# Prologue of a two-stage mixing kernel: weight additions on TensorE, a third output buffer, split loads of the mixer input, and steps of the next group begun early

## The chip, the cores and the metric

The program runs on one core of a Trainium2 chip. The core has five engines that run their own instruction queues: TensorE (PE in the profile; PEld is its weight load), VectorE (DVE), ScalarE (ACT), GpSimd (POOL) and SyncE (SP). SP, ACT and POOL issue the DMAs, which run on 16 DMA engines. Times are device microseconds of one execution; the metric is the median over several executions. Lower is better.

## The reference

Two blocks run one after the other on x of shape (8, 3008, 256), float32.

```python
X = np.fft.rfft(x, axis=1)                         # block 1: global filter
y = np.fft.irfft(X * (filt_r + 1j * filt_i)[None], n=3008, axis=1)
xt = y.transpose(0, 2, 1)                          # block 2: token and channel mixing
h = np.maximum(xt @ w_tok1, 0.0) @ w_tok2          # (3008, 256), (256, 3008)
u = y + h.transpose(0, 2, 1)
h2 = np.maximum(u @ w_ch1, 0.0) @ w_ch2            # (256, 1536), (1536, 256)
return u + h2
```

`filt_r` and `filt_i` are (1505, 256). x and the filters are float32; the four mixer weights arrive as float64 and are rounded to float32 on the chip.

## The kernel before

**The filter.** N = 3008 is written as 47 x 64, and the transform is done as two matmul passes. `dft(bs)` is a generator that runs it for a group of batches; one `next` is one step. Its first 12 steps per batch are `a_unit`s: load an x tile (`x_load`, two DMAs on SP), one matmul with the table `wa`, a copy to `t1` on ACT, a write to the scratch tensor `z_tmp` from ACT's queue. Then come 32 units, one per frequency row k: `b_unit` multiplies a `t2` tile (read back from `z_tmp`) by a table `wb`, and VectorE multiplies the result by the filter (L436 to L440); one step later `bi_unit` transforms back (L448), and ACT copies the result to a `t3` tile, which is written to the scratch tensor `g_tmp` (L453, L458). Rows go in chunks of KC = 2. `load(c)` fetches what chunk c needs: the table (L411, SP), the filter rows (`filt_load`, L196 to L203), and `t2` (L416, SP). For the first group it puts one copy of `filt_r` on SP and the other, with `filt_i`, on POOL; filt_r is wanted on both halves of the partitions. `load(c + 2)` is called in the unit that begins chunk c. The filter tiles are three (FB), the `wb` tiles three, the `t2` tiles three in the first group, the `t3` tiles two. PSUM bank `acc` takes every `bi_unit` of the first group.

**The weights.** Each float64 tile is staged as raw words and turned into two float32 parts whose sum is the rounded value: `halves` does a scaling on ACT (L224) and four VectorE operations (L226 to L231). For the first token weights (12 tiles, `w1_load`) the two parts are added by TensorE in two accumulating matmuls (`on_chip`, L263 and L264, with a stationary matrix that is needed anyway), and ACT copies the result (L266); these are put on the list `behind` and run two `convert` calls later. For the second token weights (16 tiles, `w2_load`, 8 of the 64 rows of n2 each) and the channel weights VectorE adds the parts (`rounded`, L252). `combine` (POOL, L311 to L315) forms the sums that the seven-product scheme of the channel matmuls needs. `convert()` moves a pipeline of tiles on: it ends tile j, scales tile j + 1 and begins the load of tile j + 4.

**The order.** All of it is written out by hand (`manual_schedule`): each engine and queue does its instructions in program order, and waits where one is not ready. The prologue runs `dft(GROUPS[0])`, which is batch 0, with a `convert` about every third step. Then it loads the mixer input of batch 0 from `g_tmp` (`t4_load`, six DMAs of 512 KB on SP, L479), converts on, and after three converts issues the token sums (96 matmuls in the trace, L485). When all 16 tiles of the second token weights are through, it does the first token tile (`u_part`: L502, L507, copy L509) and begins `mix`.

`mix` has 8 batches x 6 token tiles x 6 pairs of channel tiles = 288 items. An item has three places at which it yields. The steps of the next group's `dft` are put there: for group (1, 2) at every place while the first transforms last (`spread`), then at place 1 of each item and at place 2 of two items in three; later groups take place 1 alone. The mixer input of the next batch is loaded when the group's steps are done, and its token sums come at item 32 of the 36 of a batch. The channel matmuls are L542, L558 and L576; VectorE's work on them is L520, ACT's L545 and L563.

`t4p` has seven buffers; the 12 staged tiles of the first token weights use it first, then the six tiles of mixer input.

## Time and profile before

| what | value |
|---|---|
| median of 7 runs | 2603.8 us (2600.55 to 2605.8) |
| profiled execution, its own time | 2604.55 us |
| its span | 2602.6 us |
| first transforms of batch 0 | about 5 to 36 us |
| filter units of batch 0 | 45.9 to 133.2 us |
| token sums of batch 0 | 139.8 to 163.8 us |
| first channel matmul (L542) | 178.3 us |
| first transforms of batches 1 and 2 | 182.8 to about 265 us |
| their filter units | about 278 to 480 us |

The page gives the busy share of each engine, then the span in 40 slices with one digit for each engine. A stage is read from its own window: which engine is full, and who waits for whom. "Busy" of PE is matmuls whose ends are modelled. A matmul of the program appears as two records (L388 x2). L numbers are lines of the kernel before.

### The profile page before, as it was taken

What the parts mean: (1) busy time and instruction counts of PE and PEld (TensorE: products, weight loads), DVE (VectorE), ACT (ScalarE), POOL (GpSimd) and SP (SyncE); (2) the same over time, 40 slices, a digit from 0 to 9 for tenths busy, and PEclk for the clock granted to TensorE, in tenths of its full rate; (3) what the DMA queues carried; (4) which work ended last, traced back from release to release, by engine and by line L of the source; (5) the groups of instructions that cost most, each with busy time, mean ns of one, the idle gap of its engine ahead of it and who ended that gap; (6) DMA issues with size and microseconds to landing.
All of it is one profiled execution on the core that took longest, in us unless ns stands there. A gap on an engine that the chain in (4) does not pass through costs nothing.

```text
span 2602.6 us, 31550 instructions
## 1 busy us (share of the span) xinstructions
PE 2509.3 (96%) x10928; PEld 2000.2 (77%) x10928; DVE 1804.6 (69%) x3461; ACT 678.5 (26%) x1325; POOL 521.2 (20%) x951
## 2 busy tenths in 40 slices
PE   6878999999999999999999999999999999999998
PEld 2456666788878777888787877788888888888887
DVE  3797788746666888646567688845678586647676
ACT  2223222222321222212232222212222122212222
POOL 3533111211121111211212021121121121211212
PEclk8989999999999999999999999999999999999999
DMA  8765333312232322202332223211322111000001
GB/s 236 222 192 182 119 110 110 108 42 90 85 100 65 88 83 65 90 9 91 95 102 85 64 79 89 75 33 58 94 77 85 51 51 54 24 9 8 17 11 22
DMA packets 158104, 212.89 MB, mean 82 GB/s; under 512 B 35012, under 2 KB 106383, under 8 KB 157945
## 3 DMA queue, kind: packets, MB, share of 16 engines
q1 hardware_dynamic: 85897, 120.34, 15.6%
q0 software_dynamic: 30656, 39.92, 6.2%
q10 hardware_dynamic: 41392, 50.62, 5.8%
q8 instruction: 86, 1.41, 0.2%
q14 instruction: 73, 0.60, 0.1%
HBM read 135.77 MB, written 74.97 MB: 81 GB/s over the span
## 4 chain that ended last, share of the span: by engine, by line
PE 80%; DVE 12%; DMA 4%; issue 2%; ACT 1%; POOL 0%; SPq 0%; ACTq 0%; DVEq 0%; POOLq 0%
PE ps_po L576 28%; PE ps_pg L542 16%; PE ps_pg L558 12%; PE ps_b L485 3%; PE ps_acc L502 3%; PE ps_b L502 3%; PE ps_acc L485 2%; DVE t L520 2%; DVE hh L520 2%; PE ps_acc L448 2%; PE ps_acc L507 2%; PE ps_b L507 2%; PE ps_b L423 1%; PE ps_acc L388 1%; PE ps_acc L423 1%
## 5 line engine op out<-in xcount | busy, mean ns | idle before, releaser
L520 DVE TENSOR_TENSOR hh<-ps_pg,s 128x512 f32<-128x512 f32 (+3 forms) x864 | 482.7, 586 | 629.3 <-ACT s L545 628.7
L621 POOL DMA_DIRECT2D out_dram<-r x757 | 411.4, 552 | 1949.1 <-ACT hh L563 917.7
L563 ACT ACTIVATE hh<-hh 128x512 f32<-128x512 f32 (+1 forms) x576 | 348.2, 623 | 1111.6 <-DVE hh L520 1111.6
L576 PE MATMUL ps_po<-t,wc 128*128 128x256 f32 (+1 forms) x2304 | 535.5, 375 | 3.6 <-DVE t L520 2.2
L576 PEld LDWEIGHTS ps_po<-t,wc 128*128 128x128 f32 x2304 | 434.4, 190 | 130.2 <-issue 52.8
L542 PE MATMUL ps_pg<-v,wc 128*128 128x256 f32 (+1 forms) x1728 | 413.7, 375 | 2.6 <-POOL wc L314 2.4
L576 PE MATMUL ps_po<-hh,wc 128*128 128x256 f32 (+1 forms) x1728 | 413.0, 375 | 0.5 <-POOL wc L315 0.3
L542 PEld LDWEIGHTS ps_pg<-v,wc 128*128 128x128 f32 x1728 | 326.8, 190 | 43.8 <-DVE v L520 3.9
L576 PEld LDWEIGHTS ps_po<-hh,wc 128*128 128x128 f32 x1728 | 327.5, 190 | 39.2 <-ACT s L545 1.2
L558 PE MATMUL ps_pg<-u,wc 128*128 128x256 f32 (+1 forms) x1152 | 293.5, 377 | 5.1 <-DVE hh L520 4.8
L520 DVE TENSOR_TENSOR t<-t,hh 128x256 f32<-128x256 f32 (+1 forms) x576 | 242.9, 422 | 19.8
L558 PEld LDWEIGHTS ps_pg<-u,wc 128*128 128x128 f32 x1152 | 215.5, 190 | 43.0 <-DVE hh L520 16.7
L520 DVE TENSOR_TENSOR s<-ps_pg,hh 128x512 f32<-128x512 f32 (+1 forms) x288 | 196.1, 681 | 30.3 <-DVE hh L520 0.5
L520 DVE TENSOR_TENSOR t<-hh 128x512 f32<-128x512 f32 (+1 forms) x288 | 192.3, 668 | 0.6 <-ACT hh L563 0.6
L542 PE MATMUL ps_pg<-u,wc 128*128 128x256 f32 (+1 forms) x576 | 170.4, 378 | 2.0 <-DVE hh L520 2.0
L558 PE MATMUL ps_pg<-v,wc 128*128 128x256 f32 (+1 forms) x576 | 168.8, 375 | 0.0
L545 ACT COPY s<-ps_pg 128x256 f32<-128x256 f32 (+1 forms) x288 | 106.0, 368 | 145.4 <-PE ps_pg L542 138.3
L542 PEld LDWEIGHTS ps_pg<-u,wc 128*128 128x128 f32 x576 | 102.7, 191 | 21.5 <-issue 9.2
L558 PEld LDWEIGHTS ps_pg<-v,wc 128*128 128x128 f32 x576 | 108.6, 190 | 13.2
L485 PE MATMUL ps_b<-t,w 128*128 128x256 f32 x480 | 107.7, 387 | 7.7 <-DMA t<-g_tmp 6.6
L485 PEld LDWEIGHTS ps_b<-t,w 128*128 128x128 f32 x480 | 93.1, 194 | 21.8 <-DMA t<-g_tmp 7.0
L448 PE MATMUL ps_acc<-p,wb 128*96 128x256 f32 (+1 forms) x256 | 95.6, 473 | 7.2 <-DVE p L440 5.6
(87 smaller groups left out, 2230.1 us busy)
## 6 DMA issues: line engine op xcount, KB each, us to landing
z_tmp<-t ACTq DMA_DIRECT2D x96, 256.0 KB
t<-z_tmp SPq DMA_DIRECT2D x128, 192.0 KB
g_tmp<-t ACTq DMA_DIRECT2D x128, 192.0 KB
t<-g_tmp SPq DMA_DIRECT2D x48, 512.0 KB
x<-in_x_dram SPq DMA_DIRECT2D x184, 128.0 KB
out_dram<-r POOLq DMA_DIRECT2D x698, 32.0 KB, 1.8
wb<-wbi_t SPq DMA_DIRECT2D x80, 224.0 KB
filt<-in_filt_r_dram SPq DMA_DIRECT2D x144, 48.0 KB
```

Source lines behind the costliest of these rows:

```text
L423: nc.tensor.matmul(ps, wbs[k // WC][0:KR, k % WC, 0:P], t2s[k // KC][:, k % KC], start=True, stop=True)
L448: nc.tensor.matmul(ps[0:KR], wbs[k // WC][:, k % WC, P:], p, start=(i == 0), stop=(i == len(parts) - 1))
L485: nc.tensor.matmul(acc[:, t, :], w1[:, a, ts(t, P)], t4[b, a // TC4][:, a % TC4, :], start=(a == 0 and t == 0), stop=(a == A - 1 and t == ...
L502: nc.tensor.matmul(ps[:, 0:w], h1[:, t, ts(dh, P)], w2[:, t, ds(m * 512, w)], start=(t == 0), stop=False)
L507: nc.tensor.matmul(ps[:, ds(q * P, n)], t4[b, c][:, r, ts(dh, P)], wai[:, 0:n], start=False, stop=(q == 3))
L520: nc.vector.tensor_tensor(out=out, in0=in0, in1=in1, op=op)
L542: nc.tensor.matmul(ps[:, 0:hw], wc1[:, jp, n, :], mov, start=True, stop=True)
L545: nc.scalar.copy(out=s[:, 0], in_=g[0][:, 0, 0:hw])
L558: nc.tensor.matmul(ps[:, 0:hw], wc1[:, jp, n, :], mov, start=True, stop=True)
L563: nc.scalar.activation(out=hs, in_=hs, func=AF.Relu)
L576: nc.tensor.matmul(po[i][:, j, 0:hw], wc2[:, jp, n, :], mov, start=(jp == 0 and first == 1), stop=(jp == JP - 1 and last == 1))
L621: q.dma_start(rows[g, e, :, ds(h * A + 4 * m, n)], blocks[ts(g, CW), h, e, 0:n])
```

## The change

Most of the edits are in the prologue:

- The first six tiles of `w2_load` (BY_PE) are added by TensorE with an identity matrix (`ident`, loaded on SP into a seventh `t4p` buffer) and copied by ACT; the other ten are still added on VectorE. `w2` gets 64 unused columns (3072 for 3008), and each tile loads one column more, so one operation (384 elements) writes what took two (368 and 8); the inner step of the write is now 128 elements.
- The third tile of `t3` in the first group, for every third chunk, is the buffer of `h1`.
- In the first group `filt_r` is loaded once, on POOL with `filt_i`; ACT copies it to the other half of the partitions (`filt_double`), one unit ahead of its chunk.
- The `t2` load is issued before the table and filter loads; tables and filters of chunks 0 and 1 are issued at first transforms 5 and 8.
- The mixer input comes in two parts: partitions 0 to 95 (rows k below 24) during the last six steps of the filter, the other 32 after it, behind the identity and four x DMAs of the next group.
- Four first transforms of group (1, 2) are done before `mix`: two beside the conversions ahead of the token sums, two after the first token tile.
- The token sums come after four more converts, not three, and after all six TensorE additions.
- The last two converts of the prologue are interleaved with the two halves of the first token tile; `combine` of the first channel weights runs for each pair `jp` by itself, not for two at once.
- The steps of group (1, 2) behind its first transforms take place 2 in every second item, not in two of three.

```diff
--- before.py
+++ after.py
@@ -43,6 +43,9 @@
 CB = P // CW
 MT = 6
 NG = 8
+LAST_STEP = NXC + 2 + K2
+EARLY_ROWS = 96
+BY_PE = 6
 EARLY = 12
 GROUPS = ((0,), (1, 2), (3, 4), (5, 6), (7,))
 
@@ -132,6 +135,7 @@
     wa_np, wai_np, wbi_np = _make_tables()
     wa_d = nc.inline_tensor(wa_np, name="wa_t").ap()
     wai_d = nc.inline_tensor(wai_np, name="wai_t").ap()
+    ident_d = nc.inline_tensor(np.eye(P, dtype=np.float32), name="ident_t").ap()
     wait_d = nc.inline_tensor(np.ascontiguousarray(wai_np.T), name="wait_t").ap()
     wbi_d = nc.inline_tensor(wbi_np, name="wbi_t").ap()
 
@@ -180,7 +184,8 @@
 
     filts = [glob.tile([P, 2, KC, D], FP32, name="filt%d" % i) for i in range(FB)]
     w1 = glob.tile([P, A, DT], FP32, name="w1")
-    w2 = glob.tile([P, TC, N], FP32, name="w2")
+
+    w2 = glob.tile([P, TC, A * P], FP32, name="w2")
 
     wc1 = glob.tile([P, JP, 7, P], FP32, name="wc1")
     wc2 = glob.tile([P, JP, 7, P], FP32, name="wc2")
@@ -190,9 +195,11 @@
     def raw(src, row, ap):
         return bass.AP(tensor=src.tensor, offset=src.offset + row * D, ap=ap)
 
-    def filt_load(c, queues):
+    def filt_load(c, first):
         t, k0 = filts[c % FB], c * KC
-        for q, (src, i, p0) in zip(queues, ((filt_r, 0, 0), (filt_r, 0, HALF), (filt_i, 1, HALF))):
+
+        q = nc.gpsimd if first else nc.sync
+        for src, i, p0 in ((filt_r, 0, 0), (filt_i, 1, HALF)) + (() if first else ((filt_r, 0, HALF),)):
             q.dma_start(t[p0:p0 + A, i], raw(src, k0, [[64 * D, A], [D, KC], [1, D]]))
             lo = p0 + 32
             if k0 == 0:
@@ -202,6 +209,10 @@
             for j0, n in ((0, 16), (16, A - 1 - 16)):
                 q.dma_start(t[lo + j0:lo + j0 + n, i, k - k0:KC, :],
                             raw(src, 64 * (j0 + 1) - k, [[64 * D, n], [-D, k0 + KC - k], [1, D]]))
+
+    def filt_double(c):
+        t = filts[c % FB]
+        nc.scalar.copy(out=t[HALF:P, 0], in_=t[0:HALF, 0])
 
 
 
@@ -253,15 +264,17 @@
 
 
     ended = [0]
+    ident = []
     behind, banks = [], ["po%d" % i for i in range(4)]
 
     def on_chip(stat, top, rest, n, parts):
         banks.append(banks.pop(0))
 
         def f(tag=banks[0]):
-            ps = bank(tag)[:, 0:n]
-            nc.tensor.matmul(ps, stat, top, start=True, stop=False)
-            nc.tensor.matmul(ps, stat, rest, start=False, stop=True)
+            ps = bank(tag)
+            m = ident[0] if stat is None else stat
+            nc.tensor.matmul(ps[:, 0:n], m, top, start=True, stop=False)
+            nc.tensor.matmul(ps[:, 0:n], m, rest, start=False, stop=True)
             for src, dst in parts:
                 nc.scalar.copy(out=dst, in_=src(ps))
 
@@ -289,21 +302,24 @@
 
         t, g = divmod(i, N2 // NG)
         n = NG * N1
+
+        more = g + 1 < N2 // NG
         st = stage(512)
-        nc.gpsimd.dma_start(st[:, 0:n], moe_w_tok2[ts(t, P), ts(g, n)])
+        nc.gpsimd.dma_start(st[:, 0:n + more], moe_w_tok2[ts(t, P), ds(g * n, n + more)])
         yield
-
-        def some(lo, w):
-            return lambda v: v.rearrange("p (n2 n1) -> p n1 n2", n1=N1)[:, lo:lo + w, :]
-
-        w = A - 1
-        dst = w2[:, t, 0:w * P].rearrange("p (a h n2) -> p h a n2", h=2, n2=HALF)
-
-        def both(v):
-            return bass.AP(tensor=v.tensor, offset=v.offset, ap=[v.ap[0], [A, 2], [1, w], [N1, NG]])
-
-        yield from rounded(st, n, [(both, dst[:, :, :, ds(g * NG, NG)]),
-                        (some(w, 1), w2[:, t, ds(w * P + g * NG, NG)].unsqueeze(1))], False)
+        dst = w2[:, t].rearrange("p (a h n2) -> p h n2 a", h=2, n2=HALF)[:, :, ds(g * NG, NG), :]
+
+        def some(h, nh, w):
+            return (lambda v: bass.AP(tensor=v.tensor, offset=v.offset + h * A, ap=[v.ap[0], [A, nh], [N1, NG], [1, w]]),
+                    dst[:, h:h + nh, :, 0:w])
+
+        parts = [some(0, 2, A)] if more else [some(0, 1, A), some(1, 1, A - 1)]
+        if i < BY_PE:
+            h = halves(st, n + more, spare_pair())
+            yield next(h)
+            on_chip(None, *next(h), n + more, parts)
+        else:
+            yield from rounded(st, n + more, parts, False)
 
     def combine(w):
         a11, a12, s4, na22, s3, s2, s1 = (w[:, :, n, :] for n in range(7))
@@ -324,7 +340,8 @@
         yield from rounded(st, 512, [(lambda v: v.rearrange("p (i j n) -> p i j n", j=2, n=P),
                            wc1[:, 2 * q:2 * q + 2, slice(0, 5, 4) if c == 0 else slice(1, 7, 5)])], late)
         if c == DH - 1:
-            combine(wc1[:, 2 * q:2 * q + 2])
+            for jp in range(2 * q, 2 * q + 2):
+                combine(wc1[:, jp:jp + 1])
 
     def wc2_load(i):
         st = stage(512)
@@ -351,6 +368,10 @@
         s = next(it, None)
         if s:
             next(s, None)
+
+    def sum_up():
+        while behind:
+            behind.pop(0)[1]()
 
     def convert():
 
@@ -394,22 +415,30 @@
         first = bs[0] == 0
         nb = len(bs)
         todo = [(b, c) for b in bs for c in range(NXC)]
+        wbs = {}
+
+        def w_load(c):
+            if c * KC % WC == 0:
+                g = c * KC // WC
+                wbs[g] = wbp.tile([P, WC, P + KR], FP32, tag="wb", name="wb")
+                nc.sync.dma_start(wbs[g], wbi_d[:, ts(g, WC), :])
+            filt_load(c, first)
+
         ahead = 3 * XB if first else XB
         for u in todo[0:ahead]:
             x_load(*u)
+        if not first:
+            yield True
         for i, u in enumerate(todo):
+            if first and i in (5, 8):
+                w_load(i // 6)
             a_unit(*u)
             if i + ahead < len(todo):
                 x_load(*todo[i + ahead])
             yield i + 1 < len(todo)
-        wbs, t2s, t3s, prods = {}, {}, {}, {}
-
-        def load(c):
-            if c * KC % WC == 0:
-                g = c * KC // WC
-                wbs[g] = wbp.tile([P, WC, P + KR], FP32, tag="wb", name="wb")
-                nc.sync.dma_start(wbs[g], wbi_d[:, ts(g, WC), :])
-            filt_load(c, (nc.sync, nc.gpsimd, nc.gpsimd) if first else (nc.sync,) * 3)
+        t2s, t3s, prods = {}, {}, {}
+
+        def t2_load(c):
             where, tag = (sp, "s") if first and c % 3 == 2 else (t2p, "t2")
             t2s[c] = where.tile([KR, KC, nb, D], FP32, tag=tag, name="t2")
             for i, b in enumerate(bs):
@@ -448,7 +477,8 @@
                 nc.tensor.matmul(ps[0:KR], wbs[k // WC][:, k % WC, P:], p, start=(i == 0), stop=(i == len(parts) - 1))
             c, r = divmod(k, KC)
             if r == 0:
-                t3s[c] = t3p.tile([KR, KC, nb, D], FP32, tag="t3", name="t3")
+                where, tag = (h1p, "h1") if first and c % 3 == 2 else (t3p, "t3")
+                t3s[c] = where.tile([KR, KC, nb, D], FP32, tag=tag, name="t3")
 
             nc.scalar.copy(out=t3s[c][:, r].rearrange("p b (e g i) -> p b g e i", e=DH, i=CW),
                            in_=ps[0:KR].rearrange("p b (g e i) -> p b g e i", e=DH, i=CW))
@@ -457,15 +487,22 @@
                 for i, b in enumerate(bs):
                     nc.scalar.dma_start(g_d[b, ts(c, KC)].rearrange("k r d -> r k d"), t3[:, :, i, :])
 
-        load(0)
-        load(1)
+        for c in range(2):
+            t2_load(c)
+            if not first:
+                w_load(c)
         yield
         yield
+        if first:
+            filt_double(0)
         for k in range(K2 + 1):
             if k < K2:
                 b_unit(k)
                 if k % KC == 0 and k // KC + 2 < K2 // KC:
-                    load(k // KC + 2)
+                    t2_load(k // KC + 2)
+                    w_load(k // KC + 2)
+                if first and k % KC == KC - 1 and k + 1 < K2:
+                    filt_double(k // KC + 1)
             if k >= 1:
                 bi_unit(k - 1)
             yield
@@ -474,9 +511,10 @@
 
     t4 = {}
 
-    def t4_load(b, c):
-        t4[b, c] = t4p.tile([P, TC4, D], FP32, tag="t4", name="t4")
-        nc.sync.dma_start(t4[b, c], rows_of(g_d, b)[:, ts(c, TC4), :])
+    def t4_load(b, c, lo=0, hi=P):
+        if lo == 0:
+            t4[b, c] = t4p.tile([P, TC4, D], FP32, tag="t4", name="t4")
+        nc.sync.dma_start(t4[b, c][lo:hi], rows_of(g_d, b)[lo:hi, ts(c, TC4), :])
 
     def token_sums(b):
         acc = bank(free_bank()).rearrange("p (t d) -> p t d", t=TC)
@@ -727,25 +765,35 @@
                 if i in (7, 9, 11):
                     convert()
                     rounds += 1
-            elif (i - NXC) % 3 == 2:
-                convert()
-                rounds += 1
-        for _, f in behind:
-            f()
-        behind.clear()
+            else:
+                if (i - NXC) % 3 == 2:
+                    convert()
+                    rounds += 1
+
+                if LAST_STEP - 6 <= i < LAST_STEP:
+                    t4_load(0, i - LAST_STEP + 6, 0, EARLY_ROWS)
+        ident.append(t4p.tile([P, P], FP32, tag="t4", name="ident"))
+        nc.sync.dma_start(ident[0], ident_d)
+        second = dft(GROUPS[1])
+        next(second)
         for c in range(A // TC4):
-            t4_load(0, c)
+            t4_load(0, c, EARLY_ROWS)
+        sum_up()
         for i in range(rounds, A // 2 + TC * N2 // NG):
             convert()
-            if i == rounds + 2:
+            if i - rounds < XB:
+                next(second)
+            if i == A // 2 + BY_PE - 1:
+                sum_up()
                 acc = token_sums(0)
         h1s[0] = token_relu(acc)
-        for _ in range(DH):
+        for dh in range(DH):
             convert()
-        for dh in range(DH):
             u_part(0, 0, dh)
         for f in v_steps(0, 0):
             f()
+        for _ in range(XB):
+            next(second)
         group, todo, done = -1, iter(()), True
 
         def next_ready(b):
@@ -757,10 +805,10 @@
                     raise AssertionError("the filter's steps don't fit beside the mixer's")
                 group += 1
                 done = group + 1 == len(GROUPS)
-                todo = iter(()) if done else dft(GROUPS[group + 1])
+                todo = iter(()) if done else dft(GROUPS[group + 1]) if group else second
                 spread = True
 
-            if not done and (place == 1 or group == 0 and (spread or place == 2 and i % 3)):
+            if not done and (place == 1 or group == 0 and (spread or place == 2 and i % 2)):
                 spread = next(todo, "end")
                 done = spread == "end"
```

## The prediction

> **What bounds the kernel now.** I read the share of each engine first, then the busy time by stages, then the waits and the chain of the stages that are not full. The page:
>
> ```profile
> PE 2509.3 (96%) x10928; PEld 2000.2 (77%) x10928; DVE 1804.6 (69%) x3461; ACT 678.5 (26%) x1325; POOL 521.2 (20%) x951
> ...
> PE   6878999999999999999999999999999999999998
> DMA  8765333312232322202332223211322111000001
> ```
>
> TensorE is the bound from the fifth slice on. Only the start has slack. By stages (columns: window, length, busy us of PE, PEld, DVE, ACT, POOL, then clock, DMA share, GB/s):
>
> ```profile
> 44.00:134.00 90.00, 73.30 (x236) 42.30 (x236) 66.77 (x148) 24.22 (x54) 48.38 (x87) 0.91 0.78 213
> 134.00:178.00 44.00, 32.63 (x117) 24.87 (x118) 41.30 (x91) 9.99 (x18) 13.49 (x26) 0.77 0.68 218
> 178.00:298.00 120.00, 106.19 (x414) 75.19 (x413) 89.50 (x158) 40.84 (x75) 45.70 (x74) 0.99 0.51 160
> 298.00:490.00 192.00, 179.42 (x694) 124.51 (x694) 162.95 (x282) 49.41 (x93) 26.09 (x48) 1.00 0.35 101
> 490.00:2602.00 2112.00, 2095.14 (x9445) 1726.45 (x9443) 1434.65 (x2769) 542.89 (x1068) 376.50 (x693) 1.00 0.22 64
> ```
>
> From 490 us TensorE is busy 2095 of 2112 us and the change touches nothing there. So the change is worth what it takes out of the four stages before, and each has its own limit. In the filter of batch 0 (44 to 134) no engine is full. The waits of PE and of SP's queue in it (us in total, times, longest):
>
> ```profile
> PE ps_b L423 <- DMA t<-z_tmp: 16.9, 7, 6.2
> PE ps_b L423 <- DMA filt<-in_filt_r_dram: 1.6, 1, 1.6
> ```
>
> ```profile
> SPq L411 <- PE ps_acc L448: 21.9, 8, 4.5
> ...
> SPq L416 <- DMA g_tmp<-t: 6.1, 2, 3.5
> SPq L203 <- DMA g_tmp<-t: 5.2, 2, 5.0
> ```
>
> PE waits for the filter input (`t<-z_tmp`) because SP issues it last of five loads, behind the table (L411), which waits for a matmul, and behind filter rows that wait for an older write to finish. The chain shows one such step: write, then SP, then load, then PE.
>
> ```profile
> 58.33 6.09 DMA g_tmp<-t
> 64.42 0.02 issue
> 64.43 0.28 SPq L203
> 64.71 0.04 issue
> 64.76 2.74 DMA t<-z_tmp
> 67.50 0.14 issue
> 67.64 1.19 PE ps_b L423 x2
> ```
>
> From 134 to 178 VectorE is full (41.3 of 44): it converts the second token weights, and the mixer waits. Groups by shape (busy, mean ns), then two PE rows:
>
> ```profile
> L252 DVE TENSOR_TENSOR w<-both 128x368 f32<-128x368 f32 x16 | 12.7, 794 | 0.5
> L231 DVE SCALAR_TENSOR_TENSOR both<-st,both 128x376 f32<-128x376 uint32 x16 | 8.8, 551 | 0.6
> ...
> L252 DVE TENSOR_TENSOR w<-both 128x8 f32<-128x8 f32 x16 | 2.6, 163 | 0.0
> ```
>
> ```profile
> 139.77 23.98 PE L485 MATMUL ps_b<-t,w 128*128 128x256 f32 x96 [6.60 <-DMA t<-g_tmp]
> 171.42 1.22 PE L502 MATMUL ps_acc<-w,h 128*128 128x512 f32 x1 [2.10 <-DVE w L252]
> ```
>
> From 298 to 490 the filter steps of group (1, 2) run between mixer items. PE idles 12.6 us there, in items where VectorE is full:
>
> ```profile
> 322.00:334.00 12.00, 10.62 (x41) 7.12 (x40) 11.69 (x21) 3.77 (x7) 0.00 (x0) 1.00 0.37 109
> ...
> 346.00:358.00 12.00, 12.00 (x52) 8.58 (x51) 6.59 (x12) 2.77 (x5) 0.00 (x0) 1.00 0.29 91
> ```
>
> **The change part by part.** The profiled execution took 2604.55 us (span 2602.6 and 1.95 around it), 0.75 above the median of 2603.8. The sum is made against 2604.55.
>
> 1. *Tables 0 and 1 loaded during the first transforms; first filter input issued first on SP.* SP's three filter issues between the last z_tmp write (42.15) and the load at 43.28 go: 1.1 us gained. Against it, two tables (448 KB at the 252 GB/s of that stage, 1.8 us) now stand on SP between x loads. Ends +1.1 and -1.8; I take 0.
>
> 2. *Filter stage.* SP loses three filter issues per chunk of two units (1.1 us) and the filter input goes ahead of the table, so it need not wait for L411's matmul. POOL issues six filter loads per chunk as before (3.3 us). 1.4 MB of 19.1 MB (15 chunks of 94 KB) are not read. The third output buffer lets an output copy go on while a g_tmp write of 4 to 6 us is out. What can go: PE's waits above without the first start (6.2), so 10.7+1.6 = 12.3 us. What is late next: the 16 DMA engines, at shares of 0.92 to 1.03 in several 6 us windows (56 to 62, 68 to 74, 116 to 122), and VectorE, busy 66.8 of 90. I take two thirds, 8; ends 0 (DMA-bound) and 12.3. Added: 16 copies of filter rows on ACT, priced by the 128x512 copy at 0.58 each, 9.4 us on an engine busy 24 of 90. They stand before the output copy of a later unit, so a late filter load would hold that copy, then the `acc` bank, then PE (rival B). The early mixer loads (2.36 MB) stand on SP behind the last filter input, so only the last g_tmp writes meet them.
>
> 3. *From the last filter product to the mixer's start.* VectorE's path from 132.47 to 181.56. Tiles 14 to 17 lose both additions: 4 x 0.96 = 3.8 (tiles 12 and 13 lie in step 2). Ten tiles get one addition of 384 elements for two. By L252's rate it costs 794x384/368 = 829 ns and saves 0.13; by L231's contiguous rate 563 ns, and saves 0.39; one operand is strided before and after, so I take the middle, 0.26 x 10 = 2.6 (ends 1.3 and 3.9). The wait of 1.8 for the copy of u goes, as u is earlier. Against: tile 15's scaling on ACT now stands behind two copies that wait for four identity matmuls, so VectorE idles about 2.6 there (last product, two adds of 1.27 each by 512-column rows of 0.86, two copies, one scaling, less tile 14's 1.85). Sum 5.6. PE's side: twelve more matmul calls, 7.6 us, in front of the sums; PE waited 6.6 us there anyway for the mixer input, so the sums start about 4 us later, at 144, and end at 165 to 168 (21 us if all 96 go at the later rate below, 24 as before). That is close to VectorE's end of tile 27 (near 168), so I take off 0.6: 5. Ends 1.5 and 8. Identity, x and the rest of the mixer input follow one another on SP; the identity is behind 2.36 MB, 6 to 11 us at the 388 to 206 GB/s of the mixer loads after 140, begun six units, some 14 us, before the last product, so it is there. Combines in halves: first four POOL operations 2.4 us in place of 3.6, inside this sum.
>
> The sums' rows: 15 matmuls in 140 to 146 at clock 0.51, 30 in each next 6 us at 1.00, after an idle of 6.6 us. The Trainium skill ("TensorE: Matmul & The Clock Gate", What's actually happening) says the clock halves after an idle window of about 3.4 us; by it the work put into the gap would give some 3 us back, and the sums would end at 165 rather than 168.
>
> Against the change speaks "SBUF — State Buffer" of the same skill (Door 1): consecutive accesses in one 16-byte line are fast, each new line pays. The new writes step 512 bytes per element. By the rule the addition saves nothing, and step 3 would give 2.6 less; the row of 794 ns already has strided reads, and no run here shows strided writes.
>
> 4. *Four first transforms of batches 1 and 2 before the mixer.* Each is 0.86 us of PE ("PE ps_b L388 x2" in the chain), moved from a stage where PE is busy 11.3 to 12 of 12 us into gaps: 4 x 0.86 = 3.4. Ends 2 (two of them after u, partly on the path) and 3.4.
>
> 5. *Filter steps of that group 3 per 2 items, not 5 per 3.* In items where VectorE is full (four windows: 46.2 busy of 48) 6 steps replace 7; a step is four VectorE operations of 0.69, 2.8 us. VectorE there falls to 43.4, PE to 42.5; at the same 96% fill this takes 45.1, idle 2.6 in place of 3.75 per tile of tokens. Over four such: 12.6 falls to about 10. I take 3; ends 0 and 6. The steps end one item later (item 30 for 29); batch 1's input then has two items, some 16 us, for 3.1 MB, which took about 10 us at 323 GB/s: covered, 4 us spare.
>
> Sum: 0 + 8 + 5 + 3.4 + 3 = 19.4. 2604.55 - 19.4 = 2585.2; set on the median, 2584.5.
>
> **The rivals.**
> A. *The DMA engines hold the filter stage.* For: share 0.78 overall, windows above 0.9. Against: 213 GB/s on average where other stretches of the stage moved 264 and 282. Then step 2 gives 0: 2593.
> B. *The ACT copies of filter rows are late and the whole is slower.* Place: VectorE frees a filter buffer; POOL issues three loads (last begun 1.4 us later); landing 4.1 median, 6.2 at most in this stage; copy 0.6, output copy 0.4, product 0.9, next unit 0.4+0.7: 4.4 plus landing, over six units. At 2.7 us a unit (86.6 us, 45.9 to 132.5, for 32) six units are 16.2, so it binds at a landing above 11.8, and decides against the change when the stage grows by the other 11.4 us, at 3.06 us a unit: a landing of 14. At 15: 3.23 a unit, 17 us lost: 2610. Landing times speak against it.
> C. *The strided writes are dear.* If each addition cost twice 829 ns, ten lose 7.0 against the two additions of before (957 ns) where I counted 2.6 gained; step 3 falls by 9.6: 2594.
> D. *All ends are met from the good side:* 1.1+12.3+8+3.4+6 = 30.8: 2573.
> No change at all would need the start hidden by later work; but the later work is PE's own, full from 490 on, so what the start saves reaches the end.
>
> **How the numbers follow.** Main case 0.55 (2576 to 2592), A 0.17 (2593), C 0.09 (2594), D 0.08 (2573 and below), B and its like 0.11: 0.05 between 2599 and 2609, where delays cancel the gain, 0.06 above. Within 0.2% (5.2 us, what a measurement of this kernel can tell) is 2598.6 to 2609. Faster 0.89, cut to 0.87 as A and C can come together near 2604; same 0.07; slower 0.06. The range from 2571 (D) to 2599 (C and A's upper side) leaves out under 0.2.
>
> **What would show it.** Right: the mixer's first matmul near 165 (L542, now 178.3); PE's waits on `t<-z_tmp` under 8 us without the start; ACT's row copies not first in any wait; the additions between 0.56 and 0.83 us; PE at 12 of 12 in more windows of the group's filter stage; nothing changed behind it. Wrong: sums starting after 150, ACT waiting long for filter rows, or the strided additions above 1.2 us.

## The result, and the profile after

The changed kernel takes 2593.06 us (median of 12 runs, 2590.11 to 2599.15) against 2602.27 us for the kernel before (31 runs). The ratio is 0.9963, with a 95% interval of 0.9956 to 0.9971, a gain of 7.5 to 11.5 us. The forecast was 2584.5: the sign was right and the time lies in the range (2571 to 2599), but the sum of 19.4 us was twice what came, and the time lies just outside the main case (2576 to 2592).

The page of the changed kernel, shares of the engines and the slices (line numbers are those of the changed kernel from here on: L452 and L477 are the matmuls of a filter unit, L517 the mixer loads, L523 the token sums, L580 the first channel matmuls):

```profile
PE 2507.9 (97%) x10952; PEld 2001.8 (77%) x10952; DVE 1797.2 (69%) x3441; ACT 691.1 (27%) x1347; POOL 526.1 (20%) x966
...
PE   5889999999999999999999999999999999999998
DMA  8965333312332322203232232211232121100001
```

The span went from 2602.6 to 2591.5 us, 11.1 less. The same windows as before the change (length, busy us of PE, PEld, DVE, ACT, POOL, then clock, DMA share, GB/s; the last one ends earlier):

```profile
44.00:134.00 90.00, 72.09 (x242) 41.97 (x243) 65.31 (x144) 34.19 (x70) 48.55 (x88) 0.92 0.90 241
134.00:178.00 44.00, 40.37 (x154) 28.23 (x153) 38.25 (x79) 16.31 (x30) 16.26 (x30) 0.95 0.59 168
178.00:298.00 120.00, 109.21 (x425) 77.87 (x423) 96.58 (x172) 40.17 (x74) 49.20 (x84) 0.99 0.52 161
298.00:490.00 192.00, 181.75 (x722) 130.82 (x723) 162.36 (x284) 49.87 (x96) 25.98 (x48) 1.00 0.35 101
490.00:2590.00 2100.00, 2082.21 (x9386) 1716.11 (x9384) 1425.22 (x2750) 538.88 (x1060) 375.08 (x693) 1.00 0.22 63
```

Behind 490 us nothing changed. For the account I split the span at the first channel matmul on `v` (L580), called the mixer's start below: what lies before it is the prologue, what lies behind it is TensorE's own work with few gaps.

| stage | before | after | gain | step and forecast |
|---|---|---|---|---|
| first filter matmul at | 45.9 | 49.4 | -3.6 | 1: 0 (ends -1.8, +1.1) |
| filter units, first to last matmul | 87.3 | 75.1 | +12.2 | 2: 8 (0 to 12.3) |
| last filter matmul to the mixer's start | 48.2 | 52.5 | -4.3 | 3: 5 (1.5 to 8) |
| mixer's start to the end of the span | 2421.2 | 2414.5 | +6.7 | 4 and 5: 6.4 |

So the filter stage gave all that was thought possible, steps 4 and 5 together gave what they should (from one profile each; in the kernels below that have both steps the last row lies between 2414.2 and 2419.9), and the part behind the last filter product, where 5 us were to be gained, lost 4. Waits between 44 and 134 us (engine and line, what it waited for: us in total, times, longest):

```profile
PE ps_b L452 <- DMA t<-z_tmp: 9.0, 1, 9.0
...
PE ps_po L276 <- DMA ident<-ident_t: 5.8, 1, 5.8
PE ps_acc L477 <- ACT t L483: 5.3, 7, 2.0
...
ACT filt L215 <- DMA filt<-in_filt_r_dram: 3.9, 3, 2.0
```

PE waits for the filter input once, at the start, and no longer inside the stage. The new wait is the second line: TensorE waits for the 64 KB identity matrix. The same queue of SP shows why (issue time, us, then what is issued):

```profile
111.88 0.34 SPq L424 DMA_DIRECT2D wb<-wbi_t  x1
112.41 2.98 SPq L517 DMA_DIRECT2D t<-g_tmp  x6
115.50 0.49 SPq L776 DMA_DIRECT2D ident<-ident_t  x1
117.28 11.77 SPq L398 DMA_DIRECT2D x<-in_x_dram  x4
132.46 2.63 SPq L517 DMA_DIRECT2D t<-g_tmp  x6
```

The six early loads (2.36 MB) are issued at 112.4, the identity at 115.5, and the four x DMAs, spread over 11.8 us, behind them. On TensorE's and VectorE's timelines (in brackets: idle before, and what ended it):

```profile
123.85 0.67 PE L477 MATMUL ps_acc<-p,wb 128*96 128x256 f32 x2 [0.15 <-DVE p L467]
130.33 1.62 PE L276 MATMUL ps_po<-both,ident 128*128 128x377 f32 x2 [5.80 <-DMA ident<-ident_t]
...
142.94 20.88 PE L523 MATMUL ps_b<-t,w 128*128 128x256 f32 x96
```

```profile
125.20 0.55 DVE L242 SCALAR_TENSOR_TENSOR both<-st,both 128x377 f32<-128x377 uint32 x1
136.56 0.36 DVE L237 TENSOR_SCALAR both<-both 128x377 uint32<-128x377 uint32 x1 [10.80 <-ACT both L235]
```

The identity is there 14.8 us after its issue. Until then the additions on TensorE cannot run, ACT's copies of them cannot run, the scaling of the next weight tile stands behind those copies, and VectorE, which sets the end of this stage, is idle for 10.8 us. The token sums begin 18.4 us after the filter's last matmul (124.5), where 6.6 us had passed before the change.

The additions that stayed on VectorE, by shape (busy, mean ns; idle):

```profile
L263 DVE TENSOR_TENSOR w<-both 128x384 f32<-128x384 f32 x8 | 6.7, 834 | 0.3
```

### The profile page after: what moved, and what is told of

Read it like the earlier page. It is cut to its first block, busy times and chain, and to the rows that moved or that the text cites. A ratio compares the mean times of both kernels' runs of the same rounds, so it can differ in the third digit from the quotient of the medians.

```text
span 2591.5 us, 31510 instructions
## 1 busy us (share of the span) xinstructions
PE 2507.9 (97%) x10952; PEld 2001.8 (77%) x10952; DVE 1797.2 (69%) x3441; ACT 691.1 (27%) x1347; POOL 526.1 (20%) x966
## 4 chain that ended last, share of the span: by engine, by line
PE 77%; DVE 11%; issue 1%; ACT 1%; DMA 1%; POOL 1%; ACTq 0%; DVEq 0%; SPq 0%; POOLq 0%
PE ps_po L614 27%; PE ps_pg L580 16%; PE ps_pg L596 11%; PE ps_acc L540 4%; PE ps_acc L523 3%; PE ps_b L523 2%; PE ps_b L540 2%; DVE t L558 2%; DVE hh L558 2%; PE ps_acc L545 2%; DVE u L558 2%; PE ps_b L409 1%; PE ps_b L477 1%; PE ps_acc L477 1%; PE ps_b L452 1%
## 5 line engine op out<-in xcount | busy, mean ns | idle before, releaser
L580 PE MATMUL ps_pg<-v,wc 128*128 128x256 f32 (+1 forms) x1728 | 413.4, 375 | 0.2
L580 PEld LDWEIGHTS ps_pg<-v,wc 128*128 128x128 f32 x1728 | 326.9, 190 | 40.5 <-DVE v L558 3.0
L580 PE MATMUL ps_pg<-u,wc 128*128 128x256 f32 (+1 forms) x576 | 169.8, 377 | 0.0
L580 PEld LDWEIGHTS ps_pg<-u,wc 128*128 128x128 f32 x576 | 102.6, 191 | 17.2 <-issue 8.0
L540 PE MATMUL ps_acc<-w,h 128*128 128x512 f32 (+1 forms) x228 | 106.8, 590 | 3.5 <-DVE w L263 2.8
L477 PE MATMUL ps_acc<-p,wb 128*96 128x256 f32 (+1 forms) x256 | 93.9, 466 | 9.1 <-ACT t L483 5.3
L523 PE MATMUL ps_b<-t,w 128*128 128x256 f32 x384 | 83.8, 380 | 1.3 <-ACT t L483 1.3
```

Of the source, the lines that this page charges most:

```text
L477: nc.tensor.matmul(ps[0:KR], wbs[k // WC][:, k % WC, P:], p, start=(i == 0), stop=(i == len(parts) - 1))
L523: nc.tensor.matmul(acc[:, t, :], w1[:, a, ts(t, P)], t4[b, a // TC4][:, a % TC4, :], start=(a == 0 and t == 0), stop=(a == A - 1 and t == ...
L540: nc.tensor.matmul(ps[:, 0:w], h1[:, t, ts(dh, P)], w2[:, t, ds(m * 512, w)], start=(t == 0), stop=False)
L580: nc.tensor.matmul(ps[:, 0:hw], wc1[:, jp, n, :], mov, start=True, stop=True)
```

## The experiments

The theory after the result (T): the gain of the filter stage was lost because the early part of the mixer input stands ahead of the identity and of x on SP's queue. Rivals: the additions on TensorE are not worth their cost at all; the volume of the early part, not its place, does the harm; the early part itself is fine and only the identity is badly placed. Three further questions concern the sizes of steps 1, 2, 4 and 5. The kernels ran on three chips, each beside the kernel before: e1 to e4 (2603.7 us for the kernel before), e5 to e8 (2602.2) and e9, e10, e12 and e13 (2606.9). Ratios are to that. Their intervals reach some 3.5 us to each side, so between kernels of different chips a difference under about 5 us is not settled by the times alone. The other columns come from one profile of each kernel. All figures in one table; "rest" is the span behind the mixer's start:

| kernel | median us | ratio to before (95%) | first filter matmul | filter units | sums begin | mixer's start | rest |
|---|---|---|---|---|---|---|---|
| before | 2602.27 | 1 | 45.9 | 87.3 | 139.8 | 181.4 | 2421.2 |
| after | 2593.06 | 0.9963 (0.9956, 0.9971) | 49.4 | 75.1 | 142.9 | 177.0 | 2414.5 |
| e1_ident_early | 2589.33 | 0.9947 (0.9934, 0.9959) | 47.4 | 74.9 | 138.7 | 172.8 | 2415.1 |
| e2_no_pe_adds | 2591.24 | 0.9958 (0.9944, 0.9972) | 47.5 | 75.5 | 134.4 | 174.2 | 2415.0 |
| e3_whole_input | 2580.33 | 0.9913 (0.9899, 0.9926) | 47.3 | 71.8 | 129.3 | 164.1 | 2415.6 |
| e4_two_out | 2595.39 | 0.9971 (0.9959, 0.9982) | 49.9 | 78.9 | 140.4 | 175.6 | 2415.9 |
| e5_after_whole_input | 2583.55 | 0.9931 (0.9918, 0.9943) | 49.2 | 71.5 | 130.8 | 164.9 | 2419.9 |
| e6_whole_no_pe | 2583.35 | 0.9928 (0.9914, 0.9941) | 49.1 | 72.4 | 129.5 | 167.2 | 2414.2 |
| e7_whole_old_order | 2580.69 | 0.9918 (0.9905, 0.9932) | 45.5 | 71.4 | 127.0 | 161.3 | 2416.5 |
| e8_whole_filt_twice | 2593.23 | 0.9967 (0.9955, 0.9978) | 48.6 | 79.7 | 138.4 | 173.3 | 2415.8 |
| e9_whole_spacing | 2584.84 | 0.9923 (0.9911, 0.9936) | 45.8 | 72.3 | 128.3 | 163.1 | 2419.5 |
| e10_whole_no_early_steps | 2589.80 | 0.9938 (0.9926, 0.9950) | 47.7 | 71.4 | 129.2 | 163.2 | 2423.1 |
| e12_whole_tables_after | 2579.38 | 0.9899 (0.9885, 0.9912) | 45.3 | 71.2 | 126.7 | 162.0 | 2415.6 |
| e13_x_before_early | 2582.07 | 0.9913 (0.9900, 0.9927) | 47.7 | 72.8 | 132.2 | 164.7 | 2414.9 |

**Where the identity stands (e1).** The identity is loaded at the start, from ACT's queue, into a buffer of its own.

```diff
+        ident.append(p2p.tile([P, P], FP32, tag="p2", name="ident"))
         for i, _ in enumerate(dft(GROUPS[0])):
             if i == 0:
-                for t, src in ((wai_t, wait_d), (wai, wai_d)):
+                for t, src in ((wai_t, wait_d), (wai, wai_d), (ident[0], ident_d)):
...
-        ident.append(t4p.tile([P, P], FP32, tag="t4", name="ident"))
-        nc.sync.dma_start(ident[0], ident_d)
```

> The changed kernel with one thing moved: the identity matrix is loaded on ACT's queue at the start, into a buffer that nothing else uses in the prologue (the p2 tile), not on SP behind the six early mixer loads. Theory 1 (the identity's late landing at 130.3 us starves first PE, then VectorE, and eats most of what the filter stage saved): PE's wait of 5.8 us for the identity goes, VectorE's idle of 10.8 us before the fourth of the TensorE-added tiles shrinks to under 3.5, the first channel matmul moves from 176.35 to about 168.5, and the time from 2593 to about 2585. Theory 2 (the last g_tmp write and the second part of the mixer input, landing after 135, hold the token sums anyway, and VectorE's work is hidden behind them): the wait turns up elsewhere, the first channel matmul at 174 or later, the time 2590 to 2593.

Measured: 2589.33, about 4 us better than the change by the ratios. The wait for the identity is gone, but the next transfer on the queue takes its place. TensorE's timeline in e1:

```profile
124.04 0.80 PE L277 MATMUL ps_po<-both,ident 128*128 128x377 f32 x2
129.50 1.34 PE L409 MATMUL ps_b<-x,wa 128*128 128x512 f32 x2 [4.67 <-DMA x<-in_x_dram]
...
138.72 1.46 PE L523 MATMUL ps_b<-t,w 128*128 128x256 f32 x6
```

The first transform of batch 1 needs x, which also stands behind the early loads, and the remaining additions stand behind that transform on TensorE. VectorE's idle time falls from 10.8 to 8.6 us, in three pieces. Neither forecast is met: the wait did turn up elsewhere, as the second theory said, but at x and not at the token sums, and the first channel matmul (172.1) and the time lie between the two.

**No additions on TensorE (e2).** The change without them.

```diff
-BY_PE = 6
+BY_PE = 0
...
-        ident.append(t4p.tile([P, P], FP32, tag="t4", name="ident"))
-        nc.sync.dma_start(ident[0], ident_d)
...
-            if i == A // 2 + BY_PE - 1:
+            if i == A // 2 + 5:
```

> The changed kernel with no tile added by TensorE (count 6 to 0, no identity loaded); the token sums stay after the same number of conversions. Theory 1: VectorE has no wait in the section, and pays six additions of 0.83 us, four of them behind the filter (3.3 us): its path ends some 10.8 - 3.3 = 7.5 us earlier, first channel matmul about 169 to 170, time about 2586. Theory 2: the additions on TensorE are what shortens VectorE's path; without them the first channel matmul comes 3 us later than 176.35 and the time is about 2596.

Measured: 2591.24. The time lies halfway between the two forecasts, and the interval of its ratio overlaps those of the change and of e1, so in these surroundings the additions on TensorE gain nothing that the runs can tell. With them TensorE waits for the identity, without them for x:

```profile
130.04 2.04 PE L409 MATMUL ps_b<-x,wa 128*128 128x512 f32 x2 [7.05 <-DMA x<-in_x_dram]
```

It does not tell what the additions are worth without the wait; e6 is about that.

**The mixer input whole, after the filter (e3, and e5 with the identity where the change has it).**

```diff
-                if LAST_STEP - 6 <= i < LAST_STEP:
-                    t4_load(0, i - LAST_STEP + 6, 0, EARLY_ROWS)
...
-            t4_load(0, c, EARLY_ROWS)
+            t4_load(0, c)
```

e3 is e1 with this edit:

> As e1_ident_early, and the mixer input loaded in one part behind the filter, as in the kernel before. Theory 1 (the early part costs the last g_tmp writes what it saves the sums; VectorE's tiles set the section's end): the last g_tmp write is issued within 0.5 us of its copy, not 2.5, the sums start at most 2 us later than in e1, and the time is within 2 us of e1's. Rival (the early part is needed so that the sums end before VectorE's tiles): first channel matmul 3 to 5 us later than in e1, time up by as much.

e5 is the change with this edit alone:

> The changed kernel with the split of the mixer input alone undone: six loads of 512 KB behind the filter; the identity stays on SP where the change has it. Theory 1 (the early part, 2.36 MB on SP ahead of identity and x loads, is the harm; the identity's place matters only because of it): the identity lands within 4 us of its issue, PE does not wait for it, the filter's last product comes some 3 us earlier than the 124.5 of the changed kernel, first channel matmul at about 164, time 2580 to 2582, as the run with identity early and input whole. Rival (both had to go): the identity still lands late, PE waits 3 us or more, time 2585 to 2589.

Measured: 2580.33 and 2583.55. Taking the early part away gains 8.9 us on e1 (ratios 0.9947 and 0.9913 times 2603), and 8 to 9.5 us on the change. Both forecasts for e3 were wrong (within 2 us of e1, or slower): the early part was held to cost about what it saves, or to be needed. The whole input is issued at 122.0 us in e3, and the sums start at 129.3, 10.2 us after the last filter matmul, with no wait in front of them:

```profile
107.28 2.42 SPq L398 DMA_DIRECT2D x<-in_x_dram  x4
122.01 4.67 SPq L517 DMA_DIRECT2D t<-g_tmp  x6
```

```profile
118.97 0.80 PE L276 MATMUL ps_po<-both,ident 128*128 128x377 f32 x2
...
129.28 10.96 PE L523 MATMUL ps_b<-t,w 128*128 128x256 f32 x50
```

The additions and two transforms fill TensorE while the 3.1 MB arrive. VectorE idles 2.9 us in the section, about the 2.6 us that the forecast worked out for tile 15:

```profile
122.89 0.36 DVE L237 TENSOR_SCALAR both<-both 128x377 uint32<-128x377 uint32 x1 [2.88 <-ACT both L235]
```

e5 has the identity at its old place, issued at 108.9 with nothing large ahead of it, and no engine waits for it: its sums also begin 10.1 us after the last filter matmul. Its time lies between its two forecasts; by its trace the first holds, since no engine waits for the identity. The 3 us by which it is slower than e3 are not explained. (The profiled run of e5 was the slowest of its five, which its long rest in the table shows.)

**Place or volume (e13).** e1, with the x DMAs ahead of the early part, which stays.

```diff
+                if i == LAST_STEP - 7:
+                    second = dft(GROUPS[1])
+                    next(second)
                 if LAST_STEP - 6 <= i < LAST_STEP:
                     t4_load(0, i - LAST_STEP + 6, 0, EARLY_ROWS)
...
-        second = dft(GROUPS[1])
-        next(second)
```

> The mixer input in two parts as in the change, the identity at the start, and the four x DMAs issued on SP ahead of the early part instead of behind it. If the harm of the early part is its place in SP's queue (what stands behind 2.36 MB is late): TensorE no longer waits 4.7 us for x, the sums start about 133 us (138.7 with x behind), the first channel matmul stands near 167, and the time is about 2584.5. If the harm is the volume itself, moved while the filter needs the DMA engines and ahead of the last part: the filter stage stays near 75 us, the sums still start at 137 or later, and the time stays at 2588 to 2590 (2589.3 with x behind).

Measured: 2582.07, ratio 0.9913, the same as with the whole input. The early part is issued at about the same time as in e1 (107.4 for 107.1 us), and as far as the time can tell the harm is gone:

```profile
102.38 3.41 SPq L398 DMA_DIRECT2D x<-in_x_dram  x4
...
107.43 23.54 SPq L517 DMA_DIRECT2D t<-g_tmp  x12
```

```profile
122.85 1.02 PE L409 MATMUL ps_b<-x,wa 128*128 128x512 f32 x2
...
132.19 21.16 PE L523 MATMUL ps_b<-t,w 128*128 128x256 f32 x96 [1.40 <-DMA t<-g_tmp]
```

So the harm is, at least in the main, the place on the queue. The split itself gains nothing here that the runs can tell: with everything else well placed, two parts (e13) and one part (e3) give the same ratio, as TensorE has its additions to do while the whole input arrives.

**What the additions on TensorE are worth without the wait (e6).** e3 with BY_PE = 0 and no identity (the same lines as in e2).

> The kernel with the mixer input whole and no tile added by TensorE (so no identity); else as changed. If the six additions on TensorE are worth VectorE's time: VectorE pays 6 x 0.83 = 5.0 us, 3.3 of them behind the filter, but has not the idle of 2.9 us before the fourth tile; the first channel matmul is 0.5 to 2 us later than 163.6, time 2581 to 2583. If the extra matmuls and ACT copies cost as much as they save: 2578 to 2581.

Measured: 2583.35, 3 to 4 us slower than e3, with intervals that overlap. Against e7 (below), which ran on the same chip and differs from e3 only in an order that turned out to be worth nothing, it is 2.7 us slower, and the slowest run of e7 lies below the fastest of e6. The mixer starts 3.1 us later than in e3, but 1.8 of these lie ahead of the first filter matmul, where the additions have no part, and 0.5 in the filter units; behind the last filter matmul they are 0.8. So the additions are worth some 1 to 3 us. TensorE's sums in e6:

```profile
129.54 22.63 PE L523 MATMUL ps_b<-t,w 128*128 128x256 f32 x96 [6.41 <-DMA t<-g_tmp]
```

Without the additions TensorE stands idle for 6.4 us and the 96 matmuls then take 22.6 us, not 20.9. The first of them run at a lower granted clock (0.71 in the first 6 us, 1.00 in e3), as in the kernel before (0.51), where the idle was 6.6 and they took 24.0.

**What made the filter stage shorter (e4, e7, e8).** e4 is the change with two output buffers:

```diff
-                where, tag = (h1p, "h1") if first and c % 3 == 2 else (t3p, "t3")
+                where, tag = t3p, "t3"
```

> The changed kernel with two buffers for the filter output, as before. The filter stage (first L452 to last L477) takes 75.0 us in the changed kernel and took 87.3 in the one before. If the third buffer carries the stage's gain: 82 to 86 us, with waits of ACT's output copy on g_tmp writes. If the order of SP's queue and the fewer loads carry it: 75 to 78. The total follows the stage: up by 7 to 11 in the first case, by 0 to 3 in the second.

Measured: the stage takes 78.9 us for 75.1, and the time is about 2 us more, with intervals that overlap. The waits between 44 and 134 us in e4 name the cause, an output copy that stands until a write is out, and the matmul behind it:

```profile
PE ps_acc L477 <- ACT t L483: 8.3, 4, 6.7
...
ACT t L483 <- DMA g_tmp<-t: 6.6, 1, 6.6
```

It is in the main one wait, ahead of the filter's last matmuls (126.8), while the early part is on its way. The mixer starts no later for it (175.6 for 177.0 us). What the third buffer is worth without the early part was not run.

e7 is e3 with the table and filter loads ahead of the filter input again:

```diff
-                    t2_load(k // KC + 2)
                     w_load(k // KC + 2)
+                    t2_load(k // KC + 2)
```

> The kernel with the mixer input whole and the identity early (2580.3), with one more thing undone: in the filter units the table and filter loads of a chunk are issued before its filter input, as in the kernel before. If the order of SP's queue carries the filter stage's gain (input behind a table load that waits for a matmul): the stage of 71.8 us grows by 5 or more and PE waits on the filter input again; time 2585 or more. If the fewer loads and the third buffer carry it: the stage within 2 us, time within 2 us of 2580.3.

Measured: 71.4 us for 71.8, and 2580.69 for 2580.33. The order of the two is worth nothing that these runs can tell.

e8 is e3 with `filt_r` loaded twice again, one copy on SP, two loads on POOL, and no ACT copies:

```diff
-        q = nc.gpsimd if first else nc.sync
-        for src, i, p0 in ((filt_r, 0, 0), (filt_i, 1, HALF)) + (() if first else ((filt_r, 0, HALF),)):
+        for q, (src, i, p0) in zip((nc.sync, nc.gpsimd, nc.gpsimd) if first else (nc.sync,) * 3,
+                                   ((filt_r, 0, 0), (filt_r, 0, HALF), (filt_i, 1, HALF))):
...
-            filt_double(0)
...
-                    filt_double(k // KC + 1)
```

> The kernel with the mixer input whole and the identity early (2580.3), with filt_r loaded twice in the first group as before (SP and POOL) and no copies of filter rows on ACT. If the third load (3 DMAs a chunk on SP, 1.4 MB) is what held the stage: the stage of 71.8 us grows by 5 or more, and the time with it. If the ACT copies cost what the loads save: within 2 us. Rival B of the prediction (ACT copies hold the output copies): the stage shrinks and the time falls by 2 or more.

Measured: the stage takes 79.7 us for 71.8, and the time is 13 us more by the medians, 9 by the profiled spans. The waits of the stage in e8:

```profile
DVE p L465 <- DMA filt<-in_filt_i_dram: 7.7, 2, 4.0
...
PE ps_b L452 <- DMA wb<-wbi_t: 6.4, 3, 2.7
```

Filter rows and table are both late. On SP's queue the chain of the kernel before is back: issues stand until an older g_tmp write has landed, those of the table (L424) for 10.5 us, where in e3 the table is never held by such a write:

```profile
SPq L424 <- DMA g_tmp<-t: 10.5, 4, 4.4
```

e8 puts back both 1.4 MB of traffic and three issues per chunk on SP; which of the two matters more was not tried.

**The start (e12).** e3 with tables and filter rows 0 and 1 issued after the first transforms, behind the filter input.

```diff
-            if first and i in (5, 8):
-                w_load(i // 6)
...
             t2_load(c)
-            if not first:
-                w_load(c)
+            w_load(c)
```

> The kernel with the identity early and the mixer input whole, but with tables and filter rows 0 and 1 issued behind the first transforms, after the filter input, as before the change. If the early tables delay the last write and the first filter input (step 1 at its bad end): the first filter matmul at 45.5 to 46 us for 47.3, and about 1.5 us less than 2580.3. If instead the rows now come too late: the first matmul no earlier than 47, or VectorE waits 1 to 2 us for filter rows at the first product, and the time is 2580 to 2582.

Measured: 2579.38, the lowest median, ratio 0.9899. Against e3 that is 1 us by the medians and 3.6 us by the ratios; the two ran on different chips and the intervals overlap, so a gain is likely but not shown. The start is earlier, and what TensorE waits for last is now the table (lines of e12 are two lower than in the change):

```profile
45.30 1.19 PE L450 MATMUL ps_b<-t,wb 96*128 96x256 f32 x2 [6.08 <-DMA wb<-wbi_t]
```

In the twelve profiles with early tables (the change and e1 to e10 and e13) the first filter matmul stands between 45.5 and 49.9 us, at 47.7 in the middle; in the two without (before, e12) at 45.9 and 45.3. Two of the twelve (e7 at 45.5, e9 at 45.8) start as early, so one profile does not settle it.

**Steps 4 and 5 (e9, e10).** e9 is e3 with the old spacing, e10 is e9 without the four early transforms.

```diff
-            if not done and (place == 1 or group == 0 and (spread or place == 2 and i % 2)):
+            if not done and (place == 1 or group == 0 and (spread or place == 2 and i % 3)):
```

> The kernel with the identity early and the mixer input whole after the filter (2580.3), but with the steps of group (1, 2) at place 2 of two items in three, as before the change. Step 5 of the prediction (3 us, ends 0 and 6): about 2583, and TensorE idles 2 to 3 us more than the 10.5 us of that kernel between 298 and 490 us. Rival, that the spacing moves idle time without removing any: within 1 us of 2580.3.

```diff
-            if i - rounds < XB:
-                next(second)
...
-        for _ in range(XB):
-            next(second)
```

> As the kernel with the old spacing, and also without the four first transforms of batches 1 and 2 ahead of the mixer (only their x loads stay there). Step 4 of the prediction: four transforms of 0.86 us come back into a stage where TensorE is full, 3.4 us more than the kernel with the old spacing, about 2586. Rival: two of the four lie in a stretch (119 to 150 us) where TensorE is now the bound itself, so they were not free, and only the other two count: 1.7 us more, with the token sums starting 1.7 us earlier (about 127.5 us).

Measured: e9 is 2.6 us slower than e3 by the ratios (the intervals overlap) and 4.5 by the medians; the rest behind the mixer's start grows by 3.9 us (2415.6 to 2419.5). Between 298 and 490 us, where the forecast looked, TensorE idles 11.7 us for 10.5, which is 1.2 more and not 2 to 3; another 2.0 come between 250 and 298 us, where these steps already run (3.5 for 1.5). e10 is slower than e9, on the same chip, by 5.0 us (medians) or 3.9 (ratios); its rest grows by a further 3.6 us, and its mixer's start is the same (163.2 for 163.1). The rival that two of the four transforms cost time ahead of the sums is false: the sums begin 10.1 us after the last filter matmul in e10 and in e9, since without the transforms TensorE waits for VectorE's tiles. Without the two behind the first token tile it waits for POOL's `combine` (L330):

```profile
123.80 0.90 PE L276 MATMUL ps_po<-both,ident 128*128 128x377 f32 x2 [0.96 <-DVE both L238]
...
129.18 20.88 PE L523 MATMUL ps_b<-t,w 128*128 128x256 f32 x96
...
163.23 1.66 PE L580 MATMUL ps_pg<-v,wc 128*128 128x256 f32 x6 [2.03 <-POOL wc L330]
```

## Why the prediction was right and where it was wrong

**The step that failed is step 3**, forecast at +5 and measured at -4.3, and in it the sentence that the identity is behind 2.36 MB, 6 to 11 us at 388 to 206 GB/s, begun six units before the last product, "so it is there". Two terms of that sentence were wrong. The loads began at 112.4, not six units (14 us) before the last product but 11.4 us before the filter's last matmul (123.85): all six were issued in one go, because SP was held at the table load ahead of them (L424), whose wait ended at 111.9, and SP issues in program order. At the forecast's own rates the identity would still have been there between 119 and 124 us, before the filter's last matmul ended (124.5). What failed is the rate: 388 to 206 GB/s is what all queues moved together in that stretch, and SP's was only the larger part of it (3.5 of 5.0 MB between 138 and 152 us in the kernel before). Here 2.42 MB took from 112.4 to 130.3, 135 GB/s. The window 112 to 130, where the DMA share is full:

```profile
112.00:130.00 18.00, 11.81 (x42) 6.54 (x40) 11.94 (x28) 5.76 (x13) 4.67 (x9) 0.94 1.02 302
```

The 135 GB/s are less than half of these 302: of 5.44 MB in the window, 2.92 went through SP's queue, 1.92 through POOL's (weights) and 0.59 through ACT's (g_tmp writes). The Trainium skill ("DMA: Bandwidth & Descriptors", Queues, rings and completion order) says that each DMA engine takes the descriptors of one queue in order and turns between the queues that have work; both halves of that fit here, the identity's place behind 2.36 MB and the share that the queue got, and the forecast had weighed other rules but not this one. And the forecast asked only whether the identity would be in time; x, which the two transforms ahead of the sums need, stood behind the same loads, and e1, which is only about 4 us better than the change, shows that it alone keeps most of the loss.

The rest of step 3 held once the queue was put right. It put the sums 10.8 us after the last filter matmul (144 against 133.2); e3 measured 10.2, e13 11.7. The gap of VectorE at tile 15 was 2.9 us in e3 (forecast 2.6). The sums at full clock took 20.9 us, 3 less than before, at a granted clock of 1.00 where the kernel before had 0.51 in the first 6 us. That agrees with the rule on the clock (the Trainium skill, "TensorE: Matmul & The Clock Gate", What's actually happening): an idle gap that is filled gives some 3 us back. The ten remaining additions were mis-sized: 834 ns each, at the end of 829 and not in the middle of 563 and 829, so they save some 1.3 us and not 2.6. The rule that was weighed against the change (the Trainium skill, "SBUF — State Buffer", Door 1), as the forecast read it, would have the addition save nothing; it was 1.3 us off, as far as the middle I took, and on the other side. The first channel matmul, forecast near 165 us, came at 176.35. In e3 the stretch from the last filter matmul to the mixer's start is 44.9 us, 3.3 less than before, where step 3 had 5.

**Step 2** was right in kind and low in size: 12.2 us against 8, at its good end (12.3). That end was no limit either: with the whole input (e3, e5) the stage shrank by 15 to 16 us. The waits inside the stage that were named did go. The two thirds that were taken for fear of the DMA engines were not needed: in the filter units their share rose from 0.78 to 0.92 and the stage still shrank, so rival A is false. Of the three reasons that it gave, the single load of `filt_r` is worth 7.8 us of the stage (e8), the third buffer 3.9 beside the early part (e4), and the order of the filter input and the table nothing that could be told (e7). ACT's row copies take 0.62 us each and ACT waits 3.9 us for their loads in the whole stage, and without these copies the stage is longer and not shorter (e8), so rival B is false too. Step 2 also said that only the last g_tmp writes meet the early mixer loads. The profiles speak against that: the three with the early part ahead of x (after, e1, e2) have stages of 74.9 to 75.5 us, those with the whole input and the same loads 71.2 to 72.4, and in e1 VectorE waits 3.3 us for a filter row at 117.5, while the early loads move; the row comes on POOL's queue, so it shares the engines with them and not the queue. e13, with the early part behind x, lies at 72.8. How much of these 3 us is which is not settled by single profiles.

**Step 1** was taken at 0 and cost 3.6 us in the profiled run, about 2 in the middle of all profiles, at or beyond its bad end of -1.8. The last z_tmp write was issued at 38.8 us for 36.9, and the filter input 7.9 us behind it for 6.3: that would fit early loads that delay x, as was counted, and the write's landing too, which was not. But e7 has the same early loads, its last write at 36.9 and its first filter matmul at 45.5, so how much of the loss is theirs stays open. **Step 4** (3.4) is borne out: 3.6 by the rest, 3.9 by the ratios, 5.0 by the medians. **Step 5** (3) lies within the 2.6 to 4.5 us that e9 is slower than e3, though the intervals of the two overlap; TensorE's idle time between 298 and 490 us fell from 12.6 to 10.25 us with the change, where about 10 was forecast, and TensorE idles 3.2 us more in e9 than in e3 between 250 and 490, which speaks for it too.

That the range held the time is in part luck: its upper end was there for rivals A and C (2593 and 2594), and the time lies beside them, though the filter stage of A and the dear additions of C are both refuted by the rows above. The loss has a third cause that had no rival of its own. A rival on the identity and x arriving late, with some 10 us as its price, was missing.

## What to carry to other kernels

Before a large load is moved ahead on a queue, list everything that is issued behind it on that queue and who waits for it, and put the small loads that gate an engine first or on another queue: here (e13 against the change) that was worth 11 us by the medians, for no extra work. For the time until such a load lands take the rate of a stretch in which the other queues are as busy, and start from where the queue really gets to it, not from where the program calls it. And where TensorE has other work to do while the data arrives, try the load in one piece first: here splitting it bought nothing.

## What the runs showed of the hardware that was not expected

- A DMA of 64 KB landed 14.8 us after its issue behind six loads of 384 KB on the same queue. Beside these loads POOL's loads took less from issue to landing, though most are larger, but more than before them: 48 KB took 5.2 us, where the median between 95 and 112 us was 3.8. These lines give the KB of each, and the median us to landing, for the window 112 to 131 of the changed kernel:

```profile
st<-in_moe_w_tok_dram POOLq DMA_DIRECT2D x4, 377.0 KB, 9.6
filt<-in_filt_i_dram POOLq DMA_DIRECT2D x1, 48.0 KB, 5.2
filt<-in_filt_i_dram POOLq DMA_DIRECT2D x1, 32.0 KB, 6.4
```

- SP's x issues in the changed kernel themselves stood 5.8 us for a g_tmp write and 5.2 us for the mixer loads to land, although x goes into buffers of its own; what makes one transfer's issue wait for another's end was not tried. SP's own waits between 44 and 134 us:

```profile
SPq L398 <- DMA g_tmp<-t: 5.8, 1, 5.8
SPq L398 <- DMA t<-g_tmp: 5.2, 2, 3.9
```

- A write of 384 elements in steps of 512 bytes costs ScalarE as much as VectorE: 828 ns for its copy from PSUM (L279), 2.2 ns an element (VectorE's addition: 834 ns), where the contiguous 128x512 copy takes 586 ns, 1.1 an element.
